# Moving two activation transposes of a fused attention and MLP kernel from TensorE to the DMA queue

## The chip, the core and the metric

The kernel runs on one core of one Trainium2 chip. The metric is the device time of the whole kernel in microseconds (us), as the median of three runs. The times of the profile are counted from the start of its span.

## What is computed

The input is q, k and v of 4 batches, 8 heads, 768 positions and 64 channels. Each query attends to the 96 positions that end at itself and to the first 8 positions of the sequence; a bias that grows with the distance, with a slope for each head, is added. The result, arranged as 3072 rows of 512 channels, goes through a two-layer MLP with a squared ReLU between the layers.

```python
scores = scale * np.matmul(q, k.transpose(0, 1, 3, 2))
# ... keep = is_global | is_local; bias = -slopes * dist
scores = np.where(keep, scores + bias, -1000000000.0)
a = np.exp(scores - scores.max(-1, keepdims=True))
a = a / (a.sum(-1, keepdims=True) + 1e-09)
x = np.matmul(a, v)                      # -> (3072, 512)
h = x @ w_in                             # 512 -> 2048
r = np.maximum(h, 0.0)
out = (s * (r * r) + b) @ w_out          # 2048 -> 512
```

## The kernel before

The 3072 rows are cut into 12 granules of 256 rows; three granules make a batch. For each granule j the program goes through these parts, and overlaps three granules: scores and attention of j, the first MLP layer of j-1, the second of j-2. The order of the instructions is written by hand.

- `XBk(j)`, `XBq(j)`: k and q, loaded as bf16 by GpSimd's DMA queue, are transposed by two DMA transposes each, which SyncE issues in order.
- `S_mm`, `S_post`, `S_mul`: scores of a pair of heads on TensorE (PE), exponential on ScalarE, multiplication with a template of the bias on VectorE. `SS` does it for several pairs. A granule that opens a batch has 12 score matmuls for two pairs, the others 16.
- `A(j, hp)`: the product with v on PE, then a reciprocal and a multiplication on VectorE, which write the tile `xn` (rows on partitions).
- `XT_pe` or `XT_dma`: `xn` transposed to `xT` (channels on partitions).
- `P1(j, fp)`: 8 matmuls of the first layer, ReLU on ScalarE, square on ScalarE (`"act"`), on VectorE right after (default), or on VectorE when `Q(j, fp)` says so (`"late"`).
- `P2_mm(j, tb, part)`: a quarter, 4 matmuls, of the second layer for 128 rows. It is used for granules 0 to 2. From granule 3 (`W0 = 3`) the second layer is made in another way (`W_mm`, `W_sw`, `W_tw`, `W_post`).
- `wsum_part`, `wsum_hl`, `wsum_fin`: column sums of `w_out`, times b, as the constant `bvec` of the second layer.

```python
def XBq(j):
    qT[j] = qtp.tile([P, HP, GT], BF16, name="qT", tag="qT")
    for i in range(GB):
        nc.sync.dma_start_transpose(
            qT[j][:, :, i * P : (i + 1) * P],
            nat["q", j][:, i, :, :].rearrange("p h d -> p (h d)"),
        )

def XT_pe(j, eng="act", tag="pso"):
    # ... xT[j]: SBUF tile, ps: PSUM tile
    for hp in range(HP):
        for i in range(GB):
            nc.tensor.transpose(ps[:, hp, i * P : (i + 1) * P],
                                xn[j][:, i, 2 * hp : 2 * hp + 2, :], ident[:])
    if eng == "act":
        nc.scalar.copy(xT[j][:], ps[:])
    # ...

def XT_dma(j):
    xT[j] = xpool.tile([P, KC, GT], BF16, name="xT", tag="xT")
    for i in range(GB):
        nc.sync.dma_start_transpose(
            xT[j][:, :, i * P : (i + 1) * P],
            xn[j][:, i, :, :].rearrange("p h d -> p (h d)"),
        )
```

The stretch that the change touches, as it stands before:

```python
A(2, 3, "psh")
XB(3)
XB(4)
P2_sc(1, 0, 0)
P2_mm(1, 0, 0)
wsum_part(0)
XT_pe(2, "act", "av")
P2_mm(1, 0, 1)
wsum_part(1)
P2_mm(1, 0, 2)
P2_mm(0, 0, 3)
P2_raw(0, 0)
wsum_part(2)
P2_mm(0, 1, 3)
P2_raw(0, 1)
P2_mm(1, 0, 3)
P2_raw(1, 0)
pace(raw[1, 0][0:1, 0:1])
load_granule(5)
wsum_part(3)
wsum_hl()
W_tw(1, 0, 4)
W_tw(1, 4, 8)
# ...
P2b(0)                       # P2b(c): P2_mm(1, 1, c), quarters of granule 1, second block
P2b(1)
for f in range(4):
    P1(2, f, "act" if f % 2 else "late")
Q(2, 0)
Q(2, 2)
period(3, [...], (3, 1, 3, 1), wsum_fin, ((W_tw, 3, 0, 4), (W_tw, 3, 4, 8)))
# period(3) ends with wsum_fin and XT_pe(3, "act", "psh"); period(4) follows; from j = 5 on: steady(j)
```

Of the kernel before, what the change touches and what calls it, by code (L numbers as in the profile page):

```python
# [8 lines left out]
F32 = mybir.dt.float32  # L9
# [9 lines left out]
def kernel(  # L19
# [13 lines left out]
    nc = tc.nc  # L33
# [5 lines left out]
    DM = H * D  # L39
# [42 lines left out]
    def bg(j):  # L82
        return divmod(j, NGR)
# [33 lines left out]
    def load_granule(j):  # L117
        load_rows(j, "k")
        load_rows(j, "q")
        load_v(j)  # L120
# [3 lines left out]
    def pace(t):  # L124
        nc.gpsimd.tensor_copy(pdum[:], t)  # L125
# [183 lines left out]
    def XB(j, nms="kq"):  # L309
        if "k" in nms:  # L310
            XBk(j)
        if "q" in nms:
            XBq(j)
# [18 lines left out]
    def KO(j):  # L332
        b, g = bg(j)
        if g == 0:
            return
        ko = work.tile([P, HP, GB, P], BF16, name="ko", tag="ko", bufs=2)
        lo = (g * GB - 1) * P
        nc.vector.tensor_copy(
            ko[:].rearrange("p h a c -> p h (a c)"), kT[b % 2][:, :, lo : lo + GT]
        )  # L340
        nc.vector.tensor_copy(
            ko[:, :, :, 0:NG],
            kT[b % 2][:, :, 0:NG].unsqueeze(2).to_broadcast((P, HP, GB, NG)),
        )
        kos[j] = ko
# [12 lines left out]
    def VO(j):  # L358
        b, g = bg(j)
        if g == 0:  # L360
            return
        vo = work.tile([P, GB, H, VW], BF16, name="vo", tag="vo", bufs=2)
        nc.vector.tensor_copy(
            vo[:, :, :, 0:65], vaug[b % 2][:, g * GB - 1 : (g + 1) * GB - 1, :, 0:65]
        )
        nc.vector.tensor_copy(
            vo[0:NG, :, :, 0:65],
            vaug[b % 2][0:NG, 0:1, :, 0:65].to_broadcast((NG, GB, H, 65)),
        )
        vos[j] = vo  # L370
# [72 lines left out]
    def SS(j, hps, which=None):  # L443
        for hp in hps:
            S_mm(j, hp, which=which)
        for hp in hps:
            S_post(j, hp)

    def A(j, hp, tag="av", norm=True, av=None):
        b, g = bg(j)  # L450
        first = g == 0
        pt = pts.pop((j, hp))
        if j not in xn:
            xn[j] = xpool.tile([P, GB, H, D], BF16, name="xn", tag="xn", bufs=2)
        if av is None:
            av = PS[tag].tile([P, GB, 2, 65], F32, name="ps_av", tag=tag)
        for i in range(GB):
            for hi in range(2):
                h = 2 * hp + hi
                if first:  # L460
                    ops = [(i, vaug[b % 2][:, i, h, 0:65])]
                    if i == 1:
                        ops.append((2, vaug[b % 2][:, 0, h, 0:65]))
                else:
                    ops = [
                        ((0, 2)[i], vaug[b % 2][:, g * GB + i, h, 0:65]),
                        ((1, 3)[i], vos[j][:, i, h, 0:65]),
                    ]
                for n_, (c, vv) in enumerate(ops):
                    nc.tensor.matmul(  # L470
                        av[:, i, hi, :],
                        lhsT=pt[:, hi, c * P : (c + 1) * P],
                        rhs=vv,
                        start=n_ == 0,
                        stop=n_ == len(ops) - 1,
                    )
        avs[j, hp] = av
        if norm:
            A_norm(j, hp)
            flush()  # L480
# [14 lines left out]
    def XT_pe(j, eng="act", tag="pso"):  # L495
        xT[j] = xpool.tile([P, KC, GT], BF16, name="xT", tag="xT")
        ps = PS[tag].tile([P, KC, GT], BF16, name="ps_x", tag=tag)
        for hp in range(HP):
            for i in range(GB):
                nc.tensor.transpose(  # L500
                    ps[:, hp, i * P : (i + 1) * P],
                    xn[j][:, i, 2 * hp : 2 * hp + 2, :],
                    ident[:],
                )
        if eng == "act":
            nc.scalar.copy(xT[j][:], ps[:])
        else:
            nc.vector.tensor_copy(xT[j][:], ps[:])
# [19 lines left out]
# [7 lines that stand above are left out]
# [52 lines left out]
    def Q(j, fp):  # L587
        gs = late_sq.pop((j, fp))
        nc.vector.tensor_tensor(gs, gs, gs, ALU.mult)  # L589
# [18 lines left out]
        nc.vector.tensor_tensor(hl[:, 1, :], wsum[:, 0, :], hl[:, 0, :], ALU.subtract)  # L608

    def wsum_fin():  # L610
        ps = ps_h.tile([P, DM], F32, name="ps_b", tag="psh")
        for i in range(2):
            nc.tensor.matmul(ps[:], lhsT=ones_f[:], rhs=hl[:, i, :], start=i == 0, stop=i == 1)
        nc.vector.tensor_scalar_mul(bvec[:], ps[:], b_bc[:])
# [22 lines left out]
    def P2_out(j, tb):  # L637
        b, g = bg(j)
        o_sb = o_tile(j, tb)
        nc.vector.scalar_tensor_tensor(  # L640
            out=o_sb,
            in0=po[j, tb],
            scalar=s_bc[:],
            in1=bvec[:],
            op0=ALU.mult,
            op1=ALU.add,
        )
        if tb == 1:
            P2_store_all(j)

    raw = {}

# [5 lines left out]
    def P2_bias(j, tb, store=True):  # L658
        o_sb = raw[j, tb]
        nc.vector.tensor_tensor(o_sb, o_sb, bvec[:], ALU.add)  # L660
        if store:
            P2_store(j, tb)

    def P2_store_all(j):
        b, g = bg(j)
        t0 = b * S + g * GT
        nc.sync.dma_start(
            out[t0 : t0 + GT, :].rearrange("(i p) c -> p i c", p=P), o_t[j][:]
        )

    def P2_store(j, tb):
        b, g = bg(j)
# [101 lines left out]
    def W_rows(j):  # L774
        b, g = bg(j)
        t0 = b * S + g * GT
        return out[t0 : t0 + GT, :].rearrange("(p r) c -> p r c", r=2)

    def W_store(j):
        nc.sync.dma_start(W_rows(j), wt[j, "o"][:])  # L780

    def W(j, n, *sums):
        W_mm(j, n)
# [172 lines left out]
    A(2, 2)  # L956
    P2_mm(0, 1, 2)
    A(2, 3, "psh")
    XB(3)
    XB(4)  # L960
    P2_sc(1, 0, 0)
    P2_mm(1, 0, 0)
    wsum_part(0)
    XT_pe(2, "act", "av")
    P2_mm(1, 0, 1)
    wsum_part(1)
    P2_mm(1, 0, 2)
# [14 lines left out]
    def run(items, n):  # L982
        for _ in range(n):
            if items:
                f, *a = items.pop(0)
                f(*a)

    def P2b(c):
        if c == 0:
            po[1, 1] = ps_o.tile([P, DM], F32, name="ps_2", tag="pso")[:]  # L990
        P2_mm(1, 1, c)
        if c == 3:
            P2_raw(1, 1)

    def period(j, items, at, late=None, mid=()):
        SS(j, (0, 1))
        run(items, at[0])
        A(j, 0)
        run(items, at[1])
        A(j, 1, "psh")  # L1000
        run(list(mid), 100)
        SS(j, (2, 3))
        if j == 3:
            pace(pts[j, 2][0:1, 0, 0:1])
            load_granule(6)
        run(items, at[2])
        A(j, 2)
        if at[3]:
            KO(j + 1)
        run(items, at[3])  # L1010
        A(j, 3, "psh")
        if not at[3]:
            KO(j + 1)
        if late is None:
            XT_dma(j)
        if j + 1 < NJ:
            VO(j + 1)
        if j + 2 < NJ:
            XB(j + 2)
        if late is not None:  # L1020
            run(items, 1)
            late()
            XT_pe(j, "act", "psh")
        run(items, 100)

    P2b(0)
    P2b(1)
    for f in range(4):
        P1(2, f, "act" if f % 2 else "late")
    Q(2, 0)  # L1030
    Q(2, 2)
    period(
        3,
        [
            (P2b, 2),
            (P2b, 3),
            (P1, 2, 4),
            (P1, 2, 5, "act"),
            (P1, 2, 6, "act"),
            (P1, 2, 7, "act"),  # L1040
            (P2, 2, 0),
            (P2, 2, 1),
            (P2, 2, 2),
            (P2, 2, 3),
            (P2_bias, 0, 0, False),
            (P2_bias, 0, 1, False),
            (P2_store_all, 0),
        ],
        (3, 1, 3, 1),
        wsum_fin,  # L1050
        ((W_tw, 3, 0, 4), (W_tw, 3, 4, 8)),
    )

    def P1s(j, fp, n):
        P1(j, fp)
# [82 lines left out]
        r(7)  # L1138
        W_sw(m, 3)

    for j in range(4, NJ):
        m, l = j - 1, j - 2
        if l < W0:
            items = [(P1, m, 0, "act"), (P2, l, 4), (P1, m, 1), (W_tw, 2, 0, 4)]
            items += [(P2, l, 5), (P2_bias, 1, 0)]
            items += [(P1, m, 2, "late"), (P1, m, 3, "late"), (P2, l, 6), (Q, m, 2), (Q, m, 3)]
            items += [(P1, m, 4, "act"), (P2, l, 7), (P1, m, 5, "act"), (P1, m, 6), (W_tw, 4, 0, 4), (P1, m, 7), (W_sw, m, 3), (flush,), (W_tw, 4, 4, 8)]
            period(j, items, (4, 2, 3, 0), mid=((W_tw, 2, 4, 8), (P2_bias, 1, 1, False)))
        else:
            steady(j)  # L1150
    l, m = NJ - 2, NJ - 1
    r = lambda f: P1(m, f, "late")
    Q(l, 7)
# [72 lines left out]
```

The softmax here doesn't subtract the row's maximum and nothing guards it: scores larger than these inputs give would overflow.

## Time and profile before

| What | Value |
|---|---|
| Median of 3 runs | 207.62 us (207.6 to 207.8) |
| Span of the profile | 205.9 us |
| Data moved by DMA | 27.64 MB, mean 134 GB/s |
| PE transposes `ps_x` of granules 2 and 3 | 8 matmuls each, from 40.84 and 61.01 us |
| ScalarE copies `xT` of the two (L506) | 2 of 1.01 us |
| DMA transposes issued by SyncE | 18 of kT, 18 of qT, 16 of xT |
| Merged stores of a whole granule | 10 of 512 KB, 6.0 us to landing |

In the profile, PE is TensorE's matmul, PEld its weight load, DVE VectorE, ACT ScalarE, POOL GpSimd and SPq the queue of SyncE. A line such as `L552` is the line of the kernel; `out<-in` are its tiles. The ends of matmuls are modelled, so a PE that looks busy may have small holes; they show in the distances between starts. The chain that ended last is followed back from the end of the kernel: its pieces are what the time consisted of. "To landing" is the time from the issue of a DMA until its semaphore tells that the data is there. A "DMA share" is the time that packets took in a stretch, per engine and time, and it can be over 1 when packets overlap.

### The profile page before, as it was taken

To read this page: it belongs to the slowest core of one execution; us is meant where nothing else is said; L and a number is where in the kernel's file an instruction comes from. 1 tells how busy PE (TensorE), PEld (TensorE's weight loads), DVE (VectorE), ACT (ScalarE), POOL (GpSimd) and SP (SyncE) were. 2 spreads that over 40 slices of the span, in tenths; PEclk is the share of its full clock that TensorE was granted. 3 is DMA by queue.
4 is the path that set the end of the run, shared out by engine and by line. 5 is a ranking of instruction groups with operands and counts; after the bars stand their busy time and mean duration, and the time that the engine had idled before them with its cause. 6 is when DMAs were issued, how large, how long until landed. Compare 5 with 4: busy or idle time off the path is not lost.

```text
span 205.9 us, 5597 instructions
## 1 busy us (share of the span) xinstructions
PE 198.5 (96%) x2286; PEld 160.6 (78%) x2293; DVE 173.4 (84%) x415; ACT 115.9 (56%) x174; POOL 73.2 (36%) x98
## 2 busy tenths in 40 slices
PE   7988999999999999999999999999999999999993
PEld 2667776547766678988988988988988988988883
DVE  5897677699989989788799799788799799787693
ACT  5887588355878576536536536536446446424400
POOL 8993683848274019009009119019000000000000
PEclk9999999999999999999999999999999999999999
DMA  5999999999999969969999969999975140040022
GB/s 164 193 184 197 192 194 193 181 154 145 148 133 150 237 83 99 194 137 118 108 227 109 208 91 106 204 109 121 204 85 140 42 133 23 0 153 5 0 105 102
DMA packets 103962, 27.64 MB, mean 134 GB/s; under 512 B 91392, under 2 KB 102016, under 8 KB 103936
## 3 DMA queue, kind: packets, MB, share of 16 engines
q0 software_dynamic: 70976, 13.11, 83.5%
q1 hardware_dynamic: 31904, 13.64, 33.8%
q10 hardware_dynamic: 1056, 0.52, 0.9%
q8 instruction: 18, 0.29, 0.6%
q14 instruction: 8, 0.07, 0.2%
HBM read 27.26 MB, written 6.29 MB: 163 GB/s over the span
## 4 chain that ended last, share of the span: by engine, by line
PE 81%; DMA 5%; POOL 5%; DVE 4%; ACT 2%; issue 1%; SPq 0%; POOLq 0%; ACTq 0%
PE ps L552 37%; PE ps_w L735 15%; PE ps_wb L735 7%; PE ps L622 6%; PE ps_av L470 4%; PE ps_wa L735 4%; DMA w_in_bf<-in_moe_w_in_dram 4%; PE ps_s L414 4%; POOL vaug L112 2%; PE ps_2s L622 2%; DVE pt L441 2%; DMA xT<-xn 1%; DVE o_pr L660 1%; POOL w_in_bf L129 1%; ACT pt L427 1%
## 5 line engine op out<-in xcount | busy, mean ns | idle before, releaser
L552 PE MATMUL ps<-xT,w_in_bf 128*128 128x256 bf16 x768 | 96.5, 273 | 2.1 <-DMA w_in_bf<-in_moe_w_in_dram 1.2
L552 PEld LDWEIGHTS <-w_in_bf 128*128 128x128 bf16 x768 | 72.6, 98 | 13.0 <-DMA w_in_bf<-in_moe_w_in_dram 2.3
L570 ACT ACTIVATE gT<-ps 128x512 bf16<-128x512 f32 x72 | 43.1, 598 | 58.5 <-PE ps L552 56.4
L427 ACT ACTIVATE pt<-ps_s 128x1024 bf16<-128x1024 f32 (+1 forms) x48 | 43.0, 950 | 4.0 <-PE ps_s L414 4.0
L735 PEld LDWEIGHTS <-sw 128*128 128x128 bf16 x288 | 28.1, 98 | 3.4
L589 DVE TENSOR_TENSOR gT<-gT 128x512 bf16<-128x512 bf16 x73 | 27.6, 415 | 1.7 <-ACT gT L570 1.6
L112 POOL DMA_DIRECT2D vaug<-in_v_dram x24 | 21.6, 912 | 4.1 <-DMA w_out_bf<-in_moe_w_out_dram 1.7
L441 DVE TENSOR_TENSOR pt<-pt,tmpl 128x1024 bf16<-128x1024 bf16 x31 | 20.7, 686 | 2.1 <-ACT pt L427 2.1
L735 PEld LDWEIGHTS <-gT 128*128 128x128 bf16 x208 | 19.8, 98 | 3.2 <-issue 0.2
L488 DVE TENSOR_TENSOR xn<-ps_av,rc 128x256 bf16<-128x256 f32 x48 | 20.4, 424 | 1.7
L125 POOL COPY pdum<-xT 1x1 bf16<-1x1 bf16 x5 | 2.5, 509 | 50.5 <-DMA xT<-xn 50.5
L622 PE MATMUL ps<-w_out_bf,gT 128*128 128x512 bf16 x74 | 18.8, 379 | 0.4 <-issue 0.2
L735 PE MATMUL ps_w<-tw,sw 128*128 128x256 bf16 x144 | 18.7, 273 | 0.0
L745 DVE SCALAR_TENSOR_TENSOR u<-ps_w,s_bc,bvec 128x256 f32<-128x256 f32 x27 | 12.9, 479 | 6.4 <-PE ps_w L735 6.4
L470 PEld LDWEIGHTS <-pt 128*128 128x128 bf16 x352 | 15.4, 98 | 3.3 <-DVE pt L441 1.2
L568 ACT ACTIVATE gT<-ps 128x512 bf16<-128x512 f32 x23 | 13.6, 598 | 6.9 <-PE ps L552 6.7
L104 POOL DMA_DIRECT2D qnat<-in_q_dram x18 | 16.0, 904 | 2.8 <-DMA w_out_bf<-in_moe_w_out_dram 1.4
L104 POOL DMA_DIRECT2D knat<-in_k_dram x18 | 15.9, 892 | 1.8 <-issue 1.5
L470 PE MATMUL ps_av<-vaug,pt 128*128 128x65 bf16 x224 | 16.2, 193 | 0.2 <-DVE pt L441 0.2
L622 PEld LDWEIGHTS <-gT 128*128 128x128 bf16 x96 | 8.7, 97 | 8.1
L487 DVE RECIPROCAL rc<-ps_av 128x4 f32<-128x4 f32 x48 | 8.7, 181 | 6.6 <-PE ps_av L470 6.4
L414 PE MATMUL ps_s<-qT,kT 64*128 64x128 bf16 x224 | 12.5, 218 | 0.1
(102 smaller groups left out, 242.4 us busy)
## 6 DMA issues: line engine op xcount, KB each, us to landing
out_dram<-o_pr SPq DMA_DIRECT2D x10, 512.0 KB, 6.0
vaug<-in_v_dram POOLq DMA_DIRECT2D x24, 128.0 KB, 8.0
knat<-in_k_dram POOLq DMA_DIRECT2D x22, 128.0 KB, 6.5
qnat<-in_q_dram POOLq DMA_DIRECT2D x22, 128.0 KB, 8.0
w_in_bf<-in_moe_w_in_dram POOLq DMA_DIRECT2D x8, 256.0 KB, 8.3
w_out_bf<-in_moe_w_out_dram POOLq DMA_DIRECT2D x4, 512.0 KB, 9.8
out_dram<-o_pr SPq DMA_DIRECT2D x3, 256.0 KB, 2.5
raw<-in_q_dram ACTq DMA_DIRECT2D x2, 256.0 KB, 4.9
```

The source lines that it names most:

```text
L104: nc.gpsimd.dma_start(t[:, i, :, :], src[b, :, sb * P : (sb + 1) * P, :].rearrange("h p d -> p h d"))
L112: nc.gpsimd.dma_start(vaug[b % 2][:, sb, :, 0:D], v[b, :, sb * P : (sb + 1) * P, :].rearrange("h p d -> p h d"),)
L414: nc.tensor.matmul(ps[:, hi, oc * P : (oc + 1) * P], lhsT=kt[r, :], rhs=qT[j][r, hp, i * P : (i + 1) * P], start=not biased, stop=not bias ...
L427: nc.scalar.activation(pt[:, :, 0:n], ps[:, :, 0:n], ACT.Exp, scale=QSCALE)
L441: nc.vector.tensor_tensor(x, x, m.unsqueeze(2).to_broadcast((P, 2, GB, 2 * P)), ALU.mult)
L470: nc.tensor.matmul(av[:, i, hi, :], lhsT=pt[:, hi, c * P : (c + 1) * P], rhs=vv, start=n_ == 0, stop=n_ == len(ops) - 1,)
L488: nc.vector.tensor_tensor(xn[j][:, :, 2 * hp : 2 * hp + 2, :], av[:, :, :, 0:D], rc[:].to_broadcast((P, GB, 2, D)), ALU.mult,)
L552: nc.tensor.matmul(ps[:, i, :], lhsT=w_in_bf[:, kc, fc * P : (fc + 1) * P], rhs=xT[j][:, kc, :], start=(kc == 0), stop=(kc == KC - 1),)
L570: nc.scalar.activation(gs.rearrange("p f (r t) -> p f r t", r=2), ps[:].rearrange("p f (t r) -> p f r t", r=2), ACT.Relu,)
L589: nc.vector.tensor_tensor(gs, gs, gs, ALU.mult)
L622: nc.tensor.matmul(po[j, tb], lhsT=gT[j][:, fc, tb * P : (tb + 1) * P], rhs=w_out_bf[:, fc, :], start=(fc == 0), stop=(fc == FC - 1),)
L735: nc.tensor.matmul(wt[j, ps], lhsT=lhs[:, f, :], rhs=rhs[:, f, :], start=first and f == 0, stop=f == HF - 1, skip_group_check=True,)
```

## The change

The activations of granules 2 and 3 are no longer transposed on PE and copied out of PSUM by ScalarE, but by DMA as those of the later granules are. It is for taking this work off PE and ScalarE. So that other work lies between the normalisation and the first use of `xT`, the two periods around it, which were produced by the general function `period`, are written out in a new order. In the queue of SyncE the transposes of granule 2 stand between those of k and of q of granule 3. The results of granules 0 to 2 are stored for each 128 rows, and those of granules 3 and 4 in two halves. The sum `wsum_fin` uses another PSUM tile. The squares of P1(3, 0), P1(3, 4) and P1(3, 5) go from ScalarE to VectorE.

```diff
@@ wsum_fin
-        ps = ps_h.tile([P, DM], F32, name="ps_b", tag="psh")
+        ps = ps_av.tile([P, DM], F32, name="ps_b", tag="av")
@@ P2_out
-        if tb == 1:
-            P2_store_all(j)
+        t0 = b * S + g * GT + tb * P
+        nc.sync.dma_start(out[t0 : t0 + P, :], o_sb)
@@ W_store
-        nc.sync.dma_start(W_rows(j), wt[j, "o"][:])
+        if j < W0 + 2:
+            for r in range(2):
+                nc.sync.dma_start(W_rows(j)[:, r, :], wt[j, "o"][:, r, :])
+        else:
+            nc.sync.dma_start(W_rows(j), wt[j, "o"][:])
@@ after A(2, 3, "psh")
-    XB(3)
+    XBk(3)
+    XT_dma(2)
+    XBq(3)
     XB(4)
     P2_sc(1, 0, 0)
     P2_mm(1, 0, 0)
     wsum_part(0)
-    XT_pe(2, "act", "av")
@@ after W_tw(1, 4, 8): period(3) and period(4) written out
+    for c in range(3):
+        P2b(c)
+    P1(2, 0, "late")
+    P1(2, 1, "act")
+    SS(3, (0, 1))
+    P2_mm(1, 1, 3)
+    P1(2, 2, "late")
+    P2_raw(1, 1)
+    wsum_fin()
+    P1(2, 3, "act")
+    Q(2, 0)
+    P2_bias(0, 0)
+    P1(2, 4)
+    A(3, 0)
+    P1(2, 5, "act")
+    A(3, 1, "psh")
+    Q(2, 2)
+    W_tw(3, 0, 4)
+    ...                      # scores of the pairs 2 and 3 of granule 3, multiplied apart
+    W_tw(3, 4, 8)
+    pace(pts[3, 2][0:1, 0, 0:1])
+    load_granule(6)
+    P1(2, 6, "act")
+    P1(2, 7, "act")
+    P2(2, 0)
+    A(3, 2)
+    A(3, 3, "psh")
+    XT_dma(3)
+    KO(4)
+    P2(2, 1)
+    VO(4)
+    XB(5)
+    P2(2, 2)
+    P2(2, 3)
+    P2_bias(0, 1)
+    SS(4, (0, 1))
+    P2_bias(1, 0)
+    P2(2, 4)
+    P2(2, 5)
+    W_tw(2, 0, 4)
+    A(4, 0)
+    P2(2, 6)
+    A(4, 1, "psh")
+    ...                      # scores of the pairs 2 and 3 of granule 4
+    S_mul(4, 2)
+    P2_mm(2, 1, 3)
+    P1(3, 0, "late")
+    W_tw(2, 4, 8)
+    S_mul(4, 3)
+    A(4, 2)
+    P1(3, 1, "late")
+    A(4, 3, "scB")
+    XT_dma(4)
+    ...                      # KO(5), VO(5), XB(6), Q(3, 0..2), P2_bias(1, 1), P1(3, 2) to P1(3, 7),
+                             # W_tw(4, ...), W_sw(3, 3)
```

More of the change, by code (lines that the diff above doesn't have):

```diff
@@ L662, in P2_bias @@
             P2_store(j, tb)
[L664 to L669, printed above, removed]
     def P2_store(j, tb):
@@ L993, in P2b @@
             P2_raw(1, 1)
[L995 to L1029, printed above, removed]
-    Q(2, 0)
-    Q(2, 2)
[L1032 to L1052, printed above, removed]
+    for c in range(3):
+        P2b(c)
@@ new lines @@
+    P1(2, 0, "late")
[6 more added lines that the diff above has]
+    P1(2, 3, "act")
+    Q(2, 0)
+    P2_bias(0, 0)
[3 more added lines that the diff above has]
+    A(3, 1, "psh")
+    Q(2, 2)
+    W_tw(3, 0, 4)
+    for hp in (2, 3):
+        S_mm(3, hp)
+    for hp in (2, 3):
+        S_post(3, hp, mul=False)
+    S_mul(3, 2)
+    S_mul(3, 3)
+    W_tw(3, 4, 8)
+    pace(pts[3, 2][0:1, 0, 0:1])
+    load_granule(6)
@@ new lines @@
+    P1(2, 6, "act")
[19 more added lines that the diff above has]
+    A(4, 1, "psh")
+    for hp in (2, 3):
+        S_mm(4, hp)
+    for hp in (2, 3):
+        S_post(4, hp, mul=False)
+    S_mul(4, 2)
+    P2_mm(2, 1, 3)
+    P1(3, 0, "late")
+    W_tw(2, 4, 8)
@@ L1054, in P1s @@
+    S_mul(4, 3)
[3 more added lines that the diff above has]
+    XT_dma(4)
+    P2_out(2, 1)
+    Q(3, 0)
+    KO(5)
+    P1(3, 2, "late")
+    VO(5)
+    XB(6)
+    Q(3, 1)
+    P2_bias(1, 1, False)
+    P1(3, 3)
+    Q(3, 2)
+    P1(3, 4)
+    P1(3, 5)
+    W_tw(4, 0, 4)
+    P1(3, 6)
+    P1(3, 7)
+    flush()
+    W_sw(3, 3)
+    W_tw(4, 4, 8)
     def P1s(j, fp, n):
@@ L1139, in steady @@
         W_sw(m, 3)
[L1141 to L1150, printed above, removed]
+    for j in range(5, NJ):
+        steady(j)
     l, m = NJ - 2, NJ - 1
```

## The prediction

> **What bounds the kernel now.** I read the engine totals first, then the chain of work that ended last in order of time, then the SyncE queue and its landings, because the change moves a transpose from TensorE to that queue. The totals name the suspect:
>
> ```profile
> PE 198.5 (96%) x2286; PEld 160.6 (78%) x2293; DVE 173.4 (84%) x415; ACT 115.9 (56%) x174; POOL 73.2 (36%) x98
> ```
>
> TensorE's 96% alone proves little, since the end of a matmul is modelled and overlaps the next one. The chain in order of time, asked for 40 to 79 us, is better. Columns: start, length, what.
>
> ```profile
> 41.01 0.45 PE ps_x L500 x8
> 41.45 1.73 PE ps_2s L622 x8
> ...
> 47.50 3.49 PE ps L552 x32
> 50.99 0.44 PE ps_s L414 x12
> ...
> 61.18 0.45 PE ps_x L500 x8
> ...
> 65.04 1.20 DVE pt L441 x2
> 70.08 1.22 DVE pt L441 x2
> ```
>
> The two `ps_x` pieces are the two PE transposes that the change removes: both lie on the chain. The other pieces give me the price of PE work: eight 512-column matmuls are 1.73, so four (a quarter of P2 for one 128-row block) are 0.865 us; 32 256-column ones are 3.49, so a P1 of eight is 0.872. Between 41 and 62 us PE pieces follow each other with hardly a hole. From 63 to 72 the chain goes through VectorE instead (`pt`, `o_pr`, `tw`, `xn`), and only there does PE lose time. After 78 it is PE without a break to the end, so whatever is won or lost before 78 us should stand in the final time.
>
> The real holes I find from starts of neighbouring matmuls. In the PE timeline a P1 starts at 67.71 and needs 0.87, so the next could start at 68.58:
>
> ```profile
> 68.94 1.05 PE L552 MATMUL ps<-xT,w_in_bf 128*128 128x256 bf16 x8 [0.18 <-DVE xn L488]
> 71.34 0.20 PE L470 MATMUL ps_av<-vaug,pt 128*128 128x65 bf16 x1 [0.18 <-DVE pt L441]
> ```
>
> It starts at 68.94: 0.35 lost (the bracket shows less, because of the modelled end). The same reading gives 0.34 at 71.34, and 0.23 at 77.72 for `ps_wa` after the exponential. So true waits in the stage touched are about **0.9 us**. (The low PEld share of this stage is no sign of more: 512-column matmuls need few weight loads.)
>
> Now the DMA side. These are lines of the SyncE timeline (start, time to issue the pair):
>
> ```profile
> 37.18 2.62 SPq L319 DMA_TRANSPOSE kT<-knat  x2
> 41.57 2.79 SPq L327 DMA_TRANSPOSE qT<-qnat  x2
> 47.79 2.64 SPq L319 DMA_TRANSPOSE kT<-knat  x2
> ...
> 72.51 2.50 SPq L531 DMA_TRANSPOSE xT<-xn  x2
> ```
>
> Each instruction holds the queue 1.2 us. How long until the data is there differs widely. First the qT pair of 41.57, then the xT pair of 72.51, from the view of one source line in a window:
>
> ```profile
> DMA to landing us min/median/max: 7.4/7.5/7.5
> ```
>
> ```profile
> DMA to landing us min/median/max: 2.5/2.5/2.5
> ```
>
> The load of the DMA engines explains it. In this table by stage the last two columns are DMA share and GB/s:
>
> ```profile
> 45.00:50.00 5.00, 4.95 (x36) 3.42 (x36) 4.86 (x5) 2.60 (x5) 2.90 (x4) 1.00 2.26 141
> 70.00:75.00 5.00, 4.78 (x47) 3.41 (x47) 4.86 (x14) 2.44 (x5) 0.00 (x0) 1.00 0.62 165
> ```
>
> At 45 to 50 us the engines are oversubscribed (2.26) by GpSimd's loads in 128-byte pieces; a load of q issued at 31.7 took 9.8 us. A transpose there waits behind that traffic; at 70 to 75 us (0.62) it doesn't.
>
> **What the Trainium skill says.** "DMA: Bandwidth & Descriptors", section "Queues, rings and completion order", says that each DMA engine alternates between the queues that have work, packet by packet, and takes a ring's descriptors in order. The trace agrees: 7.5 us against 2.5 for one and the same form, and the second of a pair lands after the first. "Advanced Engine Details and Errata", section "X-Bar Transpose (TRN2)", says transposing DMAs are as fast as ordinary ones; that holds in the idle stretch, but is no help here, for the ordinary ones take 9.8 us. "TensorE: Matmul & The Clock Gate", Part 4, gives some 275 ns for a PE transpose in context; here eight take 0.45 us of PE, 56 ns each, because they are pipelined, so the gain per transpose is smaller than that figure. The same page, "Why this matters for your kernels", warns of PE pauses over about 3 us; the granted clock here is 1.00 in every stage, and no pause that I expect reaches 3 us.
>
> **The change part by part.**
>
> 1. Removed: two PE transposes, 2 × 0.45 = **0.90 us of PE**, all on the chain. Two ScalarE copies of 1.01 us go with them; ScalarE is at 56% and not on the chain here, so they count for nothing by themselves.
>
> 2. Squares: in period 4 the three marked for ScalarE in P1 of granule 3 (0.63 each) go to VectorE (0.42 each): +1.26 us on VectorE. The reordering spreads VectorE's work (squares moved later, the four bias additions spread out, scores' multiplications apart). If it works, of the 0.9 us of waits I give back 0.9 at best, 0.7 likely; with nothing else the kernel would come to 207.6 − 0.9 − 0.7 to 0.9 = 205.8 to 206.0.
>
> 3. Added: xT of granule 2 by DMA. xn(2) is complete at 40.82 (the last normalisation starts 40.40 and takes 0.42), so the pair issues at about 40.85 and 42.05. Ahead in the ring is the kT pair of 37.18, whose second landed at 38.5 + 7.6 = 46.1. With the 7.4 to 7.6 us of its neighbours the second xT lands at 42.05 + 7.5 = **49.5**. When does PE want it? A(2,3) ends at 39.98; nine quarter-blocks of P2 (three of block 0 of granule 1, the last two of granule 0, then 1 more and three of block 1) come before the first P1(2): 39.98 + 9 × 0.865 = **47.8**. So PE waits about 1.7 us.
>
> 4. Behind it in the same queue stands q of granule 3. Before, the second qT was issued at 43.17 and landed at 43.17 + 7.4 = 50.6, and the scores of granule 3 started at 50.92: just in time. Now its issue can't begin before the xT pair is through: 43.3 and 44.5, so it lands no earlier than 44.5 + 7.4 = 51.9; and as two more transposes of about 2 us each (landing steps in this stretch: 44.0, 46.1, 49.1, 50.6) stand ahead in the ring, rather at **53.3**. But the reordering asks for these scores earlier: after nine P2 quarters and only two P1, 47.8 + 2 × 0.872 = **49.5**. Against a schedule without waits PE is then late by 51.9 − 49.5 = 2.4 to 53.3 − 49.5 = 3.8 us. The wait of step 3 is contained in this, not added to it.
>
> 5. xT of granule 3: shifted with the lag, its issue falls near 64, its first use, P1(3,0), some seven PE blocks (0.865 each) and two score pairs later, about 7.5 us. Granule 6's loads, paced by a tile of the same period, begin then too; even at 7.5 us landing the wait would be about 1 us, and in the lull between two granules' loads there is none. I take 0.3. The kT and qT of granule 5, which go behind it on the queue, are wanted about 14 us after that issue: no wait.
>
> 6. Stores by block instead of merged, and those of granules 3 and 4 in two: some 0.4 us more of SyncE issue for each, with SyncE mostly idle and no consumer. Zero.
>
> Sum: 207.6 − 0.9 (PE) − 0.7 (waits on VectorE) + 2.4 to 3.8 (qT of granule 3) + 0.3 = 208.7 to 210.1. Since VectorE can use PE's pause to get ahead, I take the waits as wholly gone (−0.9) and settle slightly low: **209.1 us**.
>
> **Rivals.** (a) The transposes are hidden: the landing is mostly latency and adding two to the queue costs nothing. For it: the ring ran empty for a moment between the pairs. Against: queue order alone puts qT's issue 1.3 us later and the need 1.4 us earlier. If hidden: 206.0. (b) VectorE becomes the bound: it is busy 4.7 to 4.9 of every 5 us from 40 to 75 us, save 4.28 at 55 to 60, and gets 1.26 us more. Were it at its limit with no PE pause to catch up in, the gain of part 2 would be lost and 0.4 to 0.8 added: about 207. (c) The queue is worse than thought: xT(2) pushes q of granule 3, that pushes k and q of granule 4, and xT(3) lands after 7.5 us in granule 6's loads: 4.5 + 1.5 us of waits, 211.8.
>
> **Range and chances.** The lowest sum with everything kind is 206, the one I believe 208.7 to 210.1, the worst 212. Eight in ten: 206.8 to 211.0. A gain of 2% means under 203.5; the removed work and all waits together are 1.8 us, so 0.01. A loss of 2% means over 211.8, rival (c): 0.06.
>
> **What would show it.** Right: `ps_x` gone from PE; in the waits, P1's matmul or weight load waiting on the DMA of xT near 48 us, and the scores (line of `ps_s`) waiting on the DMA of qT near 50 to 53, together 2.5 to 4 us; landings of the xT pair of 40.85 near 7 us; the PE holes at 68 and 71 us gone. Wrong: scores of granule 3 starting by 50 us, xT landing in under 6 us, or the loss sitting in waits on VectorE after 60 us. My number fails most easily on the landing of one transpose.

## The result and the profile after

The changed kernel takes 211.12 us (210.65 to 211.53, 4 runs) against 207.7 us before: a ratio of 1.0164, 95% interval 1.0135 to 1.0193. Slower was expected, but 209.1 with an upper end of 211.0 was not enough. The profiled execution has a span of 207.9 us (before: 205.9); the other three have 209.0, 209.5 and 209.8, so the profile shows the mildest of the four. That execution was timed at 210.65 us, 2.75 more than its span; in the other three this difference is 1.7 to 2.0, and in the profiled execution before it is 1.85. These 0.9 us lie outside the trace, and nothing here shows what they are. The mean granted clock was 1.00 in three of the four executions and 0.992 in one, which took 211.51.

The engine totals after:

```profile
PE 198.1 (95%) x2277; PEld 159.8 (77%) x2277; DVE 174.3 (84%) x418; ACT 112.6 (54%) x169; POOL 76.9 (37%) x98
```

There is less work on PE and on ScalarE, and yet the span is longer: the difference is idle time. The chain that ended last, from 40 to 80 us (start, length, what):

```profile
42.02 1.30 SPq L531
...
43.44 1.24 SPq L327
...
44.78 7.75 DMA qT<-qnat
...
52.57 0.46 PE ps_s L414 x10
...
63.55 0.74 DVE vo L363
64.31 0.81 DVE vo L366
65.13 0.66 DVE o_pr L640
...
65.83 1.89 PE ps L622 x8
```

Where PE pieces stood before, the chain now goes through SyncE's issue of xT (L531) and of q (L327), and then through the 7.75 us until q of granule 3 has landed. A second excursion runs through VectorE to 65.8. The same two places, and the start of P1, in the timeline:

```profile
49.41 1.91 PE L552 MATMUL ps<-xT,w_in_bf 128*128 128x256 bf16 x16 [1.56 <-DVE wsum L603]
52.57 0.46 PE L414 MATMUL ps_s<-qT,kT 64*128 64x128 bf16 x10 [1.01 <-DMA qT<-qnat]
65.83 1.89 PE L622 MATMUL ps<-w_out_bf,gT 128*128 128x512 bf16 x8 [0.76 <-DVE o_pr L640]
```

Measured from start to start, the waits are 1.73, 1.21 and 0.95 us. The profile puts the first down to VectorE's `wsum`, on which P1 doesn't depend. It is the wait for xT, as the queue of SyncE shows (start, time to issue, what), with the landings of the xT pair and of q's second instruction below it:

```profile
37.11 2.77 SPq L319 DMA_TRANSPOSE kT<-knat  x2
40.79 2.53 SPq L531 DMA_TRANSPOSE xT<-xn  x2
43.44 3.39 SPq L327 DMA_TRANSPOSE qT<-qnat  x2
```

```profile
DMA to landing us min/median/max: 7.3/7.3/7.4
```

```profile
DMA to landing us min/median/max: 7.8/7.8/7.8
```

The second xT is issued at 42.02 and lands at 49.3; P1 starts at 49.41. The second q is issued at 44.78 and lands near 52.6, 2.0 us later than before; the scores start at 52.57.

### The profile page after: what moved, and what is told of

Its sections match the earlier page's. It is cut to its first block, busy times and chain, and to the rows that moved or that the text cites. A ratio compares the mean times of both kernels' runs of the same rounds, so it can differ in the third digit from the quotient of the medians.

```text
span 207.9 us, 5589 instructions
## 1 busy us (share of the span) xinstructions
PE 198.1 (95%) x2277; PEld 159.8 (77%) x2277; DVE 174.3 (84%) x418; ACT 112.6 (54%) x169; POOL 76.9 (37%) x98
## 4 chain that ended last, share of the span: by engine, by line
PE 77%; DMA 8%; POOL 5%; DVE 3%; ACT 2%; SPq 1%; issue 1%; POOLq 0%; ACTq 0%; DVEq 0%
PE ps L552 37%; PE ps_w L728 15%; PE ps_wb L728 7%; PE ps L622 5%; DMA w_in_bf<-in_moe_w_in_dram 5%; PE ps_av L470 4%; PE ps_wa L728 4%; PE ps_s L414 4%; DMA qT<-qnat 4%; POOL vaug L112 2%; POOL w_in_bf L129 2%; ACT pt L427 1%; ACT gT L570 1%; SPq L531 1%; SPq L327 1%
## 5 line engine op out<-in xcount | busy, mean ns | idle before, releaser
L570 ACT ACTIVATE gT<-ps 128x512 bf16<-128x512 f32 x72 | 43.1, 598 | 58.5 <-PE ps L552 56.5
L427 ACT ACTIVATE pt<-ps_s 128x1024 bf16<-128x1024 f32 (+1 forms) x48 | 43.1, 951 | 7.3 <-PE ps_s L414 7.3
L589 DVE TENSOR_TENSOR gT<-gT 128x512 bf16<-128x512 bf16 x74 | 28.1, 416 | 1.7 <-ACT gT L570 1.6
L125 POOL COPY pdum<-xT 1x1 bf16<-1x1 bf16 x5 | 6.2, 1234 | 46.6 <-DMA xT<-xn 46.6
L622 PE MATMUL ps<-w_out_bf,gT 128*128 128x512 bf16 x80 | 19.2, 379 | 0.8 <-DVE o_pr L640 0.8
L622 PEld LDWEIGHTS <-gT 128*128 128x128 bf16 x96 | 8.8, 98 | 9.9 <-issue 0.7
```

The source lines that it names most:

```text
L427: nc.scalar.activation(pt[:, :, 0:n], ps[:, :, 0:n], ACT.Exp, scale=QSCALE)
L570: nc.scalar.activation(gs.rearrange("p f (r t) -> p f r t", r=2), ps[:].rearrange("p f (t r) -> p f r t", r=2), ACT.Relu,)
L622: nc.tensor.matmul(po[j, tb], lhsT=gT[j][:, fc, tb * P : (tb + 1) * P], rhs=w_out_bf[:, fc, :], start=(fc == 0), stop=(fc == FC - 1),)
```

## The experiments

The runs below were made on other chips. The kernel before takes 209.0 to 209.2 us there, and every ratio is to the kernel before on the same chip. "Changed" means the changed kernel.

| Run | What differs | Ratio to before (95%) |
|---|---|---|
| b_dma2 | before, xT of granule 2 by DMA | 1.0189 (1.0131 to 1.0246) |
| a_again | changed | 1.0191 (1.0142 to 1.0240) |
| a_again2 | changed | 1.0140 (1.0092 to 1.0187) |
| a_pe2 | changed, granule 2 on PE | 1.0055 (1.0023 to 1.0086) |
| a_pe23 | changed, both on PE | 1.0029 (1.0004 to 1.0054) |
| a_qfirst | changed, q ahead of xT | 1.0414 (1.0344 to 1.0483) |
| a_paced4 | changed, loads of granule 4 later | 1.0123 (1.0086 to 1.0160) |
| a_vo | changed, VO(4) later | 1.0195 (1.0154 to 1.0236) |
| a_fill | changed, pause filled | 1.0121 (1.0065 to 1.0177) |
| a_fill2 | changed, pause filled | 1.0188 (1.0128 to 1.0248) |
| b_late | before, one quarter ahead of the scores | 0.9975 (0.9955 to 0.9994) |
| b_late2 | before, two quarters ahead | 0.9984 (0.9954 to 1.0014) |
| b_bias | before, bias additions later | 0.9987 (0.9969 to 1.0005) |
| b_both | b_late and b_bias | 0.9961 (0.9942 to 0.9980) |

**The theory** was that the transposes land late because they stand behind GpSimd's loads and behind each other in SyncE's queue. There were two rivals: that the new order overloads VectorE, and that a queue with more transposes is slow whatever the load.

### The change once more: a_again

> The changed kernel once more, unaltered, for a second profile. Its first profile shows 2.0 us more span than the kernel before (207.9 against 205.9), the median of the times 3.4 us more. Queue theory (transposes land late behind GpSimd's loads): the landings scatter from run to run, so this profile shows a span of 209 to 210 with longer waits on xT of granule 2 and qT of granule 3 (together 4 us rather than 2.9). Rival (VectorE): the extra lies in waits on VectorE after 60 us. Time 210.6 to 211.5.

Measured: 212.4 us, with a span of 210.8 in the profile, both above what was expected. The queue of SyncE, the longest wait of PE, and then the table by stage (columns: stretch, its length, busy time of PE, PEld, DVE, ACT and POOL, granted clock, DMA share, GB/s):

```profile
38.71 2.96 SPq L319 DMA_TRANSPOSE kT<-knat  x2
41.72 2.66 SPq L531 DMA_TRANSPOSE xT<-xn  x2
44.49 3.32 SPq L327 DMA_TRANSPOSE qT<-qnat  x2
```

```profile
PE ps L552 <- DMA xT<-xn: 2.8, 2, 2.6
```

```profile
50.00:52.00 2.00, 1.32 (x8) 1.04 (x9) 1.93 (x4) 0.00 (x0) 1.73 (x2) 0.74 1.93 148
52.00:54.00 2.00, 2.00 (x12) 1.16 (x11) 1.04 (x2) 0.60 (x1) 1.41 (x2) 0.50 2.01 163
54.00:56.00 2.00, 2.00 (x22) 1.31 (x22) 0.00 (x0) 1.91 (x4) 1.22 (x2) 0.91 3.59 116
```

k of granule 3 comes later here: its load, issued at 28.6 us in both profiles, took 9.3 us to land in the first and takes 10.9 now:

```profile
DMA to landing us min/median/max: 10.9/10.9/10.9
```

So its transposes are issued at 38.71 rather than 37.11 and hold the queue until 41.7; xT, ready before that, stands behind them. It lands at 43.1 + 7.5 = 50.6 and q at 46.6 + 7.5 = 54.1. The wait for xT is 2.72 us from start to start. The transposes need no longer than in the first profile (7.5 us each against 7.3 and 7.8); it is their issue that has moved. Why the load lands later on this chip is not shown. In the table by stage the clock halves after the wait: P1's matmuls start every 0.213 us instead of 0.109. Even so that cost next to nothing here: at full clock the two P1 would have ended at 52.4, and the scores would have waited for q until 54.1 all the same, where they did start (54.13). The longer wait is on the DMA, not on VectorE, whose wait for `o_pr` is 0.9 us as before.

### Taking the parts apart: b_dma2, a_pe2, a_pe23

```diff
 # b_dma2, in the kernel before
-    XB(3)
+    XBk(3)
+    XT_dma(2)
+    XBq(3)
...
-    XT_pe(2, "act", "av")
 # a_pe2 undoes exactly this in the changed kernel; a_pe23 also
-    XT_dma(3)
...
     P2(2, 2)
+    XT_pe(3, "act", "psh")
```

> The kernel before, with nothing but xT of granule 2 by DMA, between k and q of granule 3 in the queue. Queue theory: PE has only eight quarters of the second layer ahead of the first P1, so it wants xT at 46.9 and gets it at 49.4 to 50.7, a wait of 2.5 to 3.8 us, with the clock falling after it; q of granule 3 is then late by little. Net of the 0.45 us saved 2 to 4.5 us slower than before: ratio 1.010 to 1.021. Rival (the loss of the change comes from its new order on VectorE): this kernel is 0.45 us faster than before.

> The changed kernel, but granule 2 transposed on PE again, where it was before; granule 3 stays with the DMA and the new order stays. Queue theory: q of granule 3 is issued and lands as in the kernel before (about 50.6), scores of granule 3 are wanted at about 49.9, so the waits of 1.7 and 1.2 us fall to about 0.7, PE does 0.45 more: 211.1 - 2.2 + 0.45 = 209.3, and 208.3 if the extra of the unprofiled runs goes too. VectorE theory (the new order and the three more squares cost): nothing gained, 211.1 to 211.6.

> The changed kernel with both transposes back on PE: its order, its stores and its squares alone. Queue theory: the scores of granule 3 still come about 1.4 us too early for q, but no xT stands in the queue; with the wait of 0.95 us for the output of granule 2 and without the waits of before at 68 and 71 us the ratio to before is 1.002 to 1.008. Rival (the order itself is what costs): as the changed kernel, 1.015 or more.

The DMA transpose of granule 2 alone loses as much as the whole change (1.0189); with it undone 1.0055 remains, and with both undone 1.0029. In b_dma2 the first P1 starts 3.37 us late. The waits name VectorE for it; but the second xT, issued near 42.8, lands near 50.1, and P1 starts at 50.30:

```profile
PE ps L552 <- DVE wsum L606: 3.2, 1, 3.2
```

```profile
50.30 5.17 PE L552 MATMUL ps<-xT,w_in_bf 128*128 128x256 bf16 x32 [3.21 <-DVE wsum L606]
```

That the two losses are equal is in part chance. In b_dma2 the clock falls as well (0.51 and 0.64 from 50 to 54 us), and there it costs: four P1 stand ahead of the scores, not two, and take 5.1 us instead of 3.49, with q landed at 53.7 and the scores starting only at 55.40. That is 1.6 us, which a_again didn't pay.

a_again and a_pe2 ran on the same chip: of the 1.91 points there, 1.36 hang on granule 2. The order with its stores and squares costs 0.3 (a_pe23); the intervals of a_pe2 and a_pe23 overlap, so what granule 3 costs is not separated from nothing. In a_pe2 and a_pe23 q still holds up the scores, by 2.2 us from start to start (0.45 + 1.80 and 0.31 + 1.85) where 0.7 was expected: no xT stands ahead of it, but the new order wants it earlier:

```profile
PE ps_s L414 <- DMA qT<-qnat: 1.9, 2, 1.6
```

```profile
PE ps_s L414 <- DMA qT<-qnat: 1.7, 1, 1.7
```

(a_pe2, then a_pe23.) That the reordering was free on VectorE is refuted in part by the 0.95 us for `o_pr`: a_pe2 has 0.93, a_pe23 has 0.48.

### The order in the queue: a_qfirst

```diff
-    XT_dma(2)
-    XBq(3)
+    XBq(3)
+    XT_dma(2)
```

> The changed kernel with q of granule 3 ahead of xT of granule 2 in the queue of SyncE. Queue theory: q lands some 2 to 3 us earlier and its wait is gone, but xT, issued 2.8 us later or more because it also waits for the load of q, lands near 52 to 53; PE waits 4 to 5 us there and its clock falls. As slow as the changed kernel or up to 2 us slower: ratio 1.017 to 1.028. Rival (only the pair in front matters and order is free): faster than the changed kernel by the 1.2 us of the wait on q.

Measured: 217.63 us, worse than expected. The longest wait of PE, and two rows of the table by stage:

```profile
PE ps L552 <- DMA xT<-xn: 8.9, 2, 7.5
```

```profile
52.00:54.00 2.00, 0.00 (x0) 0.00 (x0) 1.09 (x2) 0.00 (x0) 2.00 (x3) 0.57 2.02 163
54.00:56.00 2.00, 0.30 (x2) 0.27 (x3) 0.00 (x0) 0.00 (x0) 0.42 (x1) 0.50 1.87 122
```

xT is issued only at 46.88, since q waits for its own load, and PE stands from 48.0 to 55.7. The clock costs here too: q landed near 53, and the 16 matmuls of the two P1 take 3.5 us instead of 1.74. In this queue, whatever stands second pays for what the first waits for.

### Is it the load of the DMA engines? a_paced4

```diff
-        load_granule(4)          # among the early loads
...
     XBq(3)
+    pace(xT[2][0:1, KC - 1, GT - 1 : GT])
+    load_granule(4)
```

> The changed kernel, but GpSimd starts the loads of granule 4 only when xT of granule 2 has landed, so that the DMA engines are freer when the transposes of 41 to 46 us run. Nothing else moves. Queue theory with load as the cause: the xT pair lands in about 4 us instead of 7.4 and q of granule 3 before 50; both waits vanish: 211.1 - 2.9 = 208.2, or down to 207 if the scatter goes too. Rival (the landing is a fixed latency of a queue with several transposes in it, whatever the load): xT still lands near 49, time 211 or more.

The landings of the xT pair and of the q pair:

```profile
DMA to landing us min/median/max: 5.0/5.4/5.8
```

```profile
DMA to landing us min/median/max: 3.4/4.1/4.7
```

With GpSimd's queue emptier xT needs 5.4 us instead of 7.5 and q 4.1 instead of 7.9 (a_again, same chip): the landing is not a fixed latency. The wait for xT shrinks to 0.77 us, the one for q of granule 3 is gone. The time nevertheless falls only from 212.4 to 211.1, where 208.2 was expected, because the loads that start later now miss their own use (lines are numbered one lower in this kernel):

```profile
PE ps_s L413 <- DMA qT<-qnat: 2.3, 2, 1.5
PE ps L551 <- DMA xT<-xn: 1.8, 2, 1.2
```

The first line is now q of granule 4, near 63 to 65 us; in the second, 1.2 us are for xT of granule 4 at 81.85. Most of the gain was given back.

### The wait on VectorE: a_vo

```diff
     P2(2, 1)
-    VO(4)
     XB(5)
     P2(2, 2)
     P2(2, 3)
+    VO(4)
```

> The changed kernel, but the two copies of VO(4) on VectorE stand after the output of the first block of granule 2 instead of ahead of it. In the profile of the changed kernel the next quarter of the second layer waits 0.95 us for that output, which waits behind the copies. Theory: 0.7 to 0.9 us gained, 210.3. Rival: VectorE is full there, and the wait comes back at the attention product or the next output: less than 0.3 us gained.

`VO(4)` is two copies on VectorE, 0.74 and 0.81 us. There is no gain: 213.11 us against 212.4 for a_again on the same chip. xT landed late in the profiled execution (a wait of 4.4 us), so its time doesn't compare well, but the two waits do: the one for `o_pr` falls from 0.95 to 0.48 us from start to start, and the attention product waits instead:

```profile
PE ps_av L470 <- DVE pt L441: 0.9, 1, 0.9
```

VectorE is full at that point, as the rival had it, and moving a piece of its work moves the wait.

### What does the fallen clock cost? a_fill, a_again2, a_fill2

```diff
     for c in range(3):
         P2b(c)
+    idle(8, "av")
     P1(2, 0, "late")
```

> The changed kernel with eight extra 512-column matmuls on constants (1.73 us at full clock) on TensorE ahead of the first P1 of granule 2, where it otherwise waits for xT; their result is used by nothing. In two of the profiles so far that wait was 2.7 and 4.6 us, and after it the granted clock fell to a half for about 3 us; after waits of 1.7 and 1.8 us it stayed full. Clock theory: the pause is now under 2 us, the clock stays at 1.00, and the kernel gains 1.0 to 1.6 us against the changed kernel on the same chip state (ratio to before about 1.012 rather than 1.019), although it does more work. If the clock costs nothing: the same or up to 0.5 us slower.

> The changed kernel, unaltered, on the same chip as the next run. Ratio to before 1.016 to 1.022; mean granted clock 0.99 in most executions where the pause for xT passes some 2.5 us, 1.00 in the others.

> The changed kernel with the eight unused matmuls in the pause for xT, now beside the unaltered one on one chip. If the fallen clock makes up about 1.5 us of the loss, this one is 0.5 to 1.6 us faster than the unaltered changed kernel (those of its executions whose clock fell) and its clock is 1.00 in nearly all executions; what is left to the kernel before, 1.010 to 1.014, is the wait for the landings. If the clock is no matter, both have the same ratio.

In the profile of a_fill the clock stayed at 1.00, as expected. But beside the unaltered kernel on one chip (a_again2 and a_fill2) there is no gain: 1.0140 against 1.0188, with intervals that overlap. Nor did the filling keep the clock up every time: in three of the six executions of a_fill2 its mean is still 0.984 to 0.992. An estimate from the two intervals (their difference is 0.0048, give or take some 0.0077) rules out a gain of more than some 0.6 us, not a smaller one. More direct is that the loss is there at full clock: a_again2's executions at a mean clock of 0.997 to 1.000 took 211.7 to 212.6 us, 2.5 to 3.4 us over the 209.18 of the kernel before, and three of the first four executions of the changed kernel had 1.00. So the clock does not explain the missing 2 us. The profiles of a_again2 and a_fill2 fell on slow executions (214.96 and 216.27 us) and are left aside.

### The kernel before, and a better one: b_again, b_late, b_bias, b_both, b_late2

> The kernel before once more, for a profile on a chip of the later runs. In all kernels with a profile from there kT of granule 3 is issued at 38.4 to 39 us rather than 37.2, and q of granule 3 landed near 52.1 even with no xT in the queue. Theory: the kernel before then waits 0.8 to 1.5 us for q at the scores of granule 3 near 51 us, which its first profile did not show, and that is why it takes 209 rather than 207.7 there. Rival: no wait there, the chip is slower elsewhere.

Its queue and its longest wait, in a single execution on one of the later chips, which took 211.19 us, 2.0 more than the median there:

```profile
38.98 2.65 SPq L319 DMA_TRANSPOSE kT<-knat  x2
43.24 3.16 SPq L327 DMA_TRANSPOSE qT<-qnat  x2
```

```profile
PE ps_s L414 <- DMA qT<-qnat: 1.9, 2, 1.5
```

The loads of k and q land later here (q's second after 11.2 us instead of 9.1), and the kernel before has the wait for q itself: 2.3 us from start to start, with a fallen clock after it. In a more usual execution the wait is 1.1 us. The profile of b_bias, at 208.95 us, shows it, as nothing ahead of this stretch differs there from the kernel before:

```profile
52.19 0.46 PE L414 MATMUL ps_s<-qT,kT 64*128 64x128 bf16 x10 [0.81 <-DMA qT<-qnat]
```

The 0.3 us of margin (50.6 against 50.92) held on the first chip, where its four runs lie within 0.2 us, and doesn't hold here. So more work ahead of these scores should help:

```diff
 # b_late: P2b(2) ahead of P1(2, 0..3); b_late2: P2b(2) and P2b(3), and P1(2, 5) ahead of A(3, 0)
     P2b(1)
+    P2b(2)
 # b_bias: P2_bias(0, 0), P2_bias(0, 1) and the store of granule 0 from the end of period 3
 #         to where W_tw(2, 4, 8) stood in period 4; W_tw(2, 4, 8) to its end
```

> The kernel before, with one more quarter of the second layer of granule 1 (0.87 us of TensorE) ahead of the scores of granule 3 instead of behind them; everything else as it was. Theory: where q lands at 52 the wait at the scores shrinks by up to 0.87 us, ratio 0.996 to 0.998, and where q lands at 50.6 nothing changes. Rival: the attention product behind it now waits for the exponential, and nothing is gained: 1.000 to 1.003.

> The kernel before, with two additions of the constant vector (0.68 us each on VectorE) and the store of granule 0 moved from the end of period 3 into the middle of period 4, and half of one weight difference (0.68 us) moved to the end of period 4, so that VectorE reaches the scores of granule 4 earlier. Theory: the two waits of TensorE on VectorE near 68 and 71 us, 0.69 us together, go: ratio 0.996 to 0.998. Rival: VectorE is full until 76 us and the waits come back at the second pair of scores or at the start of the next period: 0.999 to 1.002.

> Both of these at once. If they are independent, the gains add: ratio 0.992 to 0.996, and this kernel beats both the one before and the changed one. If VectorE is the limit, 0.997 to 1.001.

> The kernel before with both remaining quarters of the second layer of granule 1 (1.73 us) ahead of the scores of granule 3, and P1 of granule 2, items 4 and 5, between these scores and the attention product. Theory: the wait for q near 51 us goes wholly: ratio 0.993 to 0.998, at least as good as with one quarter. Rival: what is gained there is lost where TensorE waits for the exponential or for a free PSUM tile: 0.997 to 1.002.

b_late gains 0.25%, though q came so late in its profile that the scores still wait 1.3 us. b_both gains 0.39%, somewhat less than expected, and beats both kernels. b_bias alone can't be told from nothing: the hole at 68 us is gone, but one of 0.41 us stands ahead of A(4, 2) instead, and the one at 71 us stayed (0.36). b_late2 is no better than b_late: it has no wait for q left in its profile, but two of 0.51 us from start to start at the attention product, which now comes too soon after the scores:

```profile
PE ps_av L470 <- DVE pt L437: 0.7, 2, 0.3
```

## Why the prediction was right and wrong

- **Direction and mechanism: right.** 0.90 us of PE work is gone, and transposes that land under load cost more than that. b_dma2 shows it for one part alone, and a_paced4 shows that the load lengthens the landings.
- **Step 3, xT of granule 2: right for the profiled execution.** A landing at 49.5 was expected, 49.3 was measured; a wait of 1.7 was expected, 1.73 was measured.
- **Step 4, q of granule 3: right for the profiled execution.** Late by 2.4 to 3.8 us was expected; the two waits are 1.73 + 1.21 = 2.9.
- **Step 2, waits on VectorE given back: failed.** The holes at 68 and 71 us are gone (0.69 us), but one of 0.95 us for `o_pr` at 65.83 took their place, and the 0.23 ahead of `ps_wa` stayed (79.70). Instead of the −0.9 that I finally took it is 0.95 − 0.69 = +0.26. The copies of VO(4) stand ahead of an output that frees the PSUM tile which the next quarters on PE write (L640, then L622 in the lines above). Rival (b), VectorE at its limit, was put at 0.4 to 0.8 us lost; this happened beside the waits on the DMA, not instead of them.
- **Step 5, xT of granule 3: right in size.** It costs 0.04 us in the first profile and 0.4 in a_again, against 0.3.
- **The sum.** With these terms it is 2.9 + 0.26 + 0.04 − 0.90 = 2.3 us, where I had 1.5; the spans differ by 2.0, so 0.3 us of the terms are not found again in the span. The failure of step 2 alone, some 1.2 us, is more than half of the 2.0 by which the median of 211.12 lies above 209.1.
- **The other failure is in steps 3 and 4: the issue taken as one number.** I let xT go out at 40.85, as soon as xn was complete, with the queue free. I named the landing of one transpose as the weakest number; it was 7.5 us again in a_again. There k's load lands 1.6 us later, kT holds the queue until 41.7, and xT is there at 50.6 and q at 54.1 instead of 49.3 and 52.6. At the second layer of granule 3 that execution is 2.0 us behind the first profile, and 1.9 of that are the 0.3 with which it came to this stage, 1.3 more at q and 0.35 at xT of granule 3. Of the 2.9 us between the two spans the rest comes later: some 0.3 before the last matmuls and 0.6 behind the last output.
- **What stays open.** The three unprofiled executions on the first chip have 1.1 to 1.9 us more span than the profiled one. That they owe it to a late issue like that of a_again is likely, not shown: they have no trace.
- **"No pause that I expect reaches 3 us": wrong.** Pauses of 2.7 to 7.7 us occur, and the clock halves after them. It costs 1.6 us in b_dma2, but it explains little of the median of the changed kernel: three of its four executions ran at a clock of 1.00.
- **"That holds in the idle stretch": not shown.** No ordinary DMA was issued between 70 and 75 us with which the 2.5 us of the transpose could be compared.

## What to carry to other kernels

Work moved from an engine to the DMA isn't free. Price a transpose by the landing that the same form has in that stretch of the trace, and ask what the queue in front of it waits for and what stands behind it. A just-in-time landing with 0.3 us of margin in one profile is no margin: leave room for the spread of the loads, which was 1.6 us here. When two engines are full in a stage, as PE and VectorE are here, work taken off one of them shows only if the other doesn't hold something that the first needs.

## What was unexpected of the hardware

The granted TensorE clock fell to 0.50 after pauses of 2.7 us (a_again) and 3.4 us (b_dma2) and during one of 7.7 us (a_qfirst), and not after 1.7 and 1.8 us (the changed kernel's first profile, a_pe2). In a_again it stayed there from 51.0 to about 54 us. In a_qfirst it was still 0.50 at 56 to 58 us, after PE had resumed at 55.7. The length of the pause alone doesn't decide: in b_again the clock fell (0.87, 0.50 and 0.78 in the stretches from 52 to 58 us) after waits of 0.6 and 1.7 us with two matmuls between them, and in a_pe2 it stayed at 1.00 through waits of 0.45 and 1.80 us with two matmuls between them.
